# Tile 1's second halves: two pairs per copy, on ScalarE and GpSimd, and a reordered opening

## The chip, the cores and the metric

The kernel runs on one core of a Trainium2 chip. The metric is the device time of one execution in microseconds; lower is better. The engines are TensorE (PE, with its weight loads PEld), VectorE (DVE), ScalarE (ACT), GpSimd (POOL) and SyncE (SP). DMAs of this kernel that cast from float32 to bfloat16 are issued by POOL.

## The reference

Sliding-window causal attention feeds a SwiGLU block:

```
q, k, v: [8 batches, 8 heads, 576, 64]
scores = q k^T / 8, kept where 0 <= i - j < 64
x = softmax(scores) v, heads side by side: [4608 tokens, 512]
out = (silu(x @ w_gate) * (x @ w_val)) @ w_out     # d_ff = 1536
```

## The kernel before, in words

The 4608 tokens are worked in nine tiles of 512. Tiles 0 to 6 and 8 are the first 512 positions of a batch, tile 7 holds the last 64 positions of all eight batches. A tile goes through scores (`scores`, line 283), exp and masks (lines 296 to 304), sums (`totals`, 316), the mix with v (`mix`, 395), scaling by the inverse sums into `xT` (`scale`, 411), twelve gate and value steps m (`gate_value`, 455), each closed by a Silu on ScalarE and a product on VectorE into `hT` (`gate_end`, 448 and 449), and the projection (464). The projection of a tile is woven between the attention steps of the next. The order on each engine is written out by hand: the schedule is manual, and each engine runs its instructions in the order of the program text.

Heads are worked in four pairs u. Scores need queries and keys with the head dimension on the partitions. `turn_q` (221) and `turn_k` (231) make them by 32x32 block transposes on VectorE. For that, the second half (32 of 64 dimensions) of every row must lie on the next 32 partitions. For tile 2 and on, the loads themselves put it there by reading everything twice (`load_q`, `load_k`). For tile 1, `load_plain` (112, 118) reads once into partitions 0 to 31 and 64 to 95 (a = 0 and 1), and `second_halves` (132) copies the other half over, one pair and one a per copy: four pairs of k on ScalarE at m = 7 to 10, then q of pairs 0 and 1 on ScalarE and VectorE after the last m, and q of pairs 2 and 3 on VectorE after four projection columns.

Tile 0, the opening, is special: its q and k come through PE transposes, and its pairs are mixed by `mix_first` (361). That helper writes small marker matmuls (374), the first of them followed by a VectorE copy `seen` (378), between the parts of its accumulation. The order there is: mix pairs 0 to 2, scale pairs 0 and 1, first parts of pair 3, gate columns 0 and 1 for m = 0 and 1, the rest of pair 3, scale pairs 2 and 3, columns 2 and 3.

POOL's queue through the opening holds two casts and then only DMA issues: the gate and value weights (`weights_gv`, 195), tile 1's k and q between them, the output weights (`weights_o`, 201), tile 1's v (`load_halves`, 166), and then tile 2's loads. Around the change the program reads, after the last m of tile 0:

```
    scores(1, 0)
    columns(0, 4)
    for u in (2, 3):
        second_halves(1, "q", u, (on_v, on_v))
        turn_q(1, u)
    scores(1, 1)
    columns(4, 7)
```

`columns(c0, c1)` projects tile 0's rows of hT chunks c0 to c1 into four PSUM banks, the same banks that gate and value steps use.

Of the kernel before, what the change touches and what calls it, by code (L numbers as in the profile page):

```python
# [17 lines left out]
def kernel(  # L18
# [11 lines left out]
    S, D, H = 576, 64, 8  # L30
# [15 lines left out]
    bank = [two[i][:, j] for i in range(2) for j in range(2)]  # L46
# [58 lines left out]
    def load_plain(t, which, us):  # L105

        q_s, k_s = staged[t]
        for a in range(2):
            hs = slice(a + 2 * us.start, a + 2 * us.stop - 1, 2)
            r = slice(64 * a, 64 * a + 32)  # L110
            if which == "q":
                nc.gpsimd.dma_start(
                    q_s[r, us],
                    q[batch(t), hs, 0:512].rearrange("u (r e) d -> r u (e d)", e=16),
                )
            else:
                for u in range(us.start, us.stop):
                    nc.gpsimd.dma_start(
                        k_s[r, :, u],
                        k[batch(t), 2 * u + a, 0:512].rearrange("(g r e) d -> r g (e d)", g=4, e=4),  # L120
                    )

    def second_halves(t, which, u, copies):

        for a in range(2):
            src, dst = slice(64 * a, 64 * a + 32), slice(64 * a + 32, 64 * a + 64)
            if which == "q":
                ap = staged[t][0][:, u].rearrange("r (e d) -> r e d", d=D)
            else:
                ap = staged[t][1][:, :, u].rearrange("r g (e d) -> r g e d", d=D)  # L130
            half_d = (Ellipsis, slice(0, 32)), (Ellipsis, slice(32, 64))
            copies[a](ap[dst][half_d[0]], ap[src][half_d[1]])  # L132

    def load_k(k_s, groups):

# [64 lines left out]
    def weights_o(c0, c1):  # L200
        nc.gpsimd.dma_start(
            wo[:, c0:c1, :],
            moe_w_out[P * c0:P * c1].rearrange("(c r) f -> r c f", r=P),
        )
# [12 lines left out]
    def turn_q(t, u):  # L217

        if u == 0:
            queries[t] = att.tile([P, 4, 512], BF16, name="qT", tag="qT")  # L220
        nc.vector.transpose(  # L221
            queries[t][:, u, :].rearrange("r (e x) -> r e x", e=16),
            staged[t][0][:, u].rearrange("r (e d) -> r e d", d=D)[:, :, 0:32],
        )
# [5 lines left out]
    def turn_k(dst, k_s, u):  # L230
        nc.vector.transpose(  # L231
            dst[:, u, :].rearrange("r (g x e) -> r g e x", g=4, e=4),
            k_s[:, :, u].rearrange("r g (e d) -> r g e d", d=D)[:, :, :, 0:32],
        )
# [31 lines left out]
    def scores(t, w):  # L266

        qT = queries[t]
        s_ps = wide(), wide()
        for j in range(8):  # L270
            if t == LAST:
                k_j = kT[t % 2 if j < 4 else 2]
                pieces = [(j, j + 1, 0, k_j, P * (j % 4) + 64),
                          (j, j + 1, 1, k_j, P * (j % 4))]
            else:
                pieces = [(j, min(8, j + 2), 0, kT[t % 2], 64 * j)]
            for lo, hi, c, src, k0 in pieces:
                for h in range(2):
                    for x in range(2):
                        slot = s_ps[h][half(x)].rearrange("r a b -> r (a b)")  # L280
                        n = hi - lo
                        o = P * j + 64 * c
                        nc.tensor.matmul(  # L283
                            slot[:, o:o + 64 * n].rearrange(
                                "r (n e y) -> r e n y", n=n, e=16
                            ),
                            src[half(h), 2 * w + x, k0:k0 + 64],
                            blocks(qT[half(h), 2 * w + x], t, lo, hi).rearrange(
                                "r e (n y) -> r e n y", n=n
                            ),  # L290
                        )
        n = 1024 if t == LAST else 960
        for h in range(2):
            E = eb[2 * w + h]
            flat = E[:].rearrange("r s z -> r (s z)")[:, 64:64 + n]
            nc.scalar.activation(  # L296
                flat, s_ps[h][:].rearrange("r a b -> r (a b)")[:, 0:n], AF.Exp, scale=0.125
            )
            nc.vector.tensor_mul(  # L299
                flat, flat, mask[:].rearrange("r j c e y -> r (j c e y)")[:, 0:n]  # L300
            )
            both = epool.tile([P, 8, 64], BF16, name="both", tag="both")
            lo = 2 if t == LAST else 0
            nc.vector.tensor_add(both[:], E[:, 1:17:2], E[:, lo:lo + 15:2])  # L304
            weights[t, w, h] = E, both
# [49 lines left out]
    def mix_first(us, banks, mark):  # L355

        def part(u, o_ps, x, m):
            r = slice(0, P) if m % 2 else half(x)
            E = weights[0, u]
            for h in range(2):  # L360
                nc.tensor.matmul(
                    blocks(o_ps[half(h)], 0, m, m + 1),
                    v1[r, m // 2 if m % 2 or not x else m // 2 - 1, 2 * u + h, :],
                    blocks(E[r, h, :], 0, m, m + 1),
                    start=m + x == 0, stop=(m, x) == (6, 1),
                )

        def parts(x, ms):
            for u, b in zip(us, banks):
                for m in ms:  # L370
                    part(u, bank[b], x, m)

        def marker():
            nc.tensor.matmul(bank[mark][0:D, 0:16], ones[:, 0:D], ones[:, 0:16])

        parts(0, (0, 2, 4, 6))
        marker()
        nc.vector.tensor_copy(seen[:], bank[mark][0:D, 0:1])
        parts(0, (1, 3, 5, 7))
        yield  # L380
        marker()
        parts(1, (2, 4, 6))
# [21 lines left out]
    def scale(t, u, o_ps):  # L404
        if u == 0:
            xT[t] = att.tile([P, 4, 512], BF16, name="xT", tag="xT")
        x, r = xT[t][:, u, :], inverse.pop((t, u))
        if t == NT - 1:
            x, o_ps = x.rearrange("r (x e) -> r x e", e=16), turned(o_ps)
            r = r.rearrange("r (x e) -> r x e", e=16)  # L410
        nc.vector.tensor_mul(x, o_ps, r)  # L411
# [20 lines left out]
    def gate_part(t, ms, tiles, c):  # L432
        for m, pair in zip(ms, tiles):
            for ps, w in zip(pair, (wg, wv)):
                nc.tensor.matmul(
                    ps[:], w[:, c, P * m:P * m + P], xT[t][:, c, :],
                    start=(c == 0), stop=(c == 3),
                )
# [171 lines left out]
    q_s = stage.tile([P, 4, 16 * D], BF16, name="q_s", tag="q")  # L610
    k_s = stage.tile([P, 4, 4, 4 * D], BF16, name="k_s", tag="k")
    staged[1] = q_s, k_s
    load_plain(1, "k", slice(0, 2))
    weights_gv(1024, 1280)
    load_plain(1, "k", slice(2, 4))
    weights_gv(1280, 1536)
    load_plain(1, "q", slice(0, 2))
    weights_o(0, 4)
    load_plain(1, "q", slice(2, 4))
    weights_o(4, 8)  # L620
    weights_o(8, 12)
    load_halves(nc.gpsimd, vb[1], 1)
# [23 lines left out]
    scores_first(3)  # L646
    weigh_first(3)
    log2, inv2 = sums_first(2, 6)
    for _ in mix_first(range(3), (0, 1, 4), 7):
        pass  # L650
    log2()
    inv2()
# [1 line left out]
    log3()  # L654
    inv3()
    pairs = [(bank[2], bank[3]), (bank[0], bank[1])]
    for u in range(2):
        scale(0, u, bank[u])
    late = mix_first((3,), (5,), 6)
    next(late)  # L660
    for c in range(2):
        gate_part(0, (0, 1), pairs, c)
    for _ in late:
        pass
    for u in (2, 3):
        scale(0, u, bank[u + 2])
    for c in range(2, 4):
# [2 lines left out]
    for m in range(12):  # L670
        if m < 2:
            gate_end(0, m, pairs[m])
        else:
            gate_value(0, m)
        if m == 2:
            for x in range(2):
                for c in range(2):
                    nc.vector.tensor_copy(
                        mask[half(x), 0, c],
                        tri[half(x), x ^ c].rearrange("r (y e) -> r e y", e=16),  # L680
                    )
            for i in (1, 2, 4):
                nc.vector.tensor_copy(mask[:, i:2 * i], mask[:, 0:i])
            for E in eb:
                nc.vector.memset(E[:, 0], 0.0)
        if 7 <= m < 11:
            second_halves(1, "k", m - 7, (on_a, on_a))
            turn_k(kT[1], staged[1][1], m - 7)
    for u in range(2):
        second_halves(1, "q", u, (on_a, on_v))  # L690
        turn_q(1, u)

    set_exp()
    tiles = [out_tile(), d_tile(), out_tile(), d_tile()]
# [1 line left out]
    def columns(c0, c1):  # L696
        project_part(0, range(4), tiles, range(c0, c1))

    scores(1, 0)
    columns(0, 4)  # L700
    for u in (2, 3):
        second_halves(1, "q", u, (on_v, on_v))
        turn_q(1, u)
    scores(1, 1)
    columns(4, 7)
    for w in range(2):
# [79 lines left out]
```

## Time and profile before

| | |
|---|---|
| median of 3 runs | 331.77 us (331.74 to 332.35) |
| the profiled execution | 331.83 us, of which the trace spans 330.1 us |
| PE busy | 316.4 us (96%) |
| VectorE, ScalarE, GpSimd busy | 223.5, 170.5, 147.8 us |
| granted PE clock, whole span | 0.995 of full speed |

Engines run beside each other, so busy times do not add up. A line L of the profile is a line of the kernel; the helpers' lines gather all calls. In views by time, the first numbers are the start, in us from the start of the span, and the duration. "[1.07 <-DVE qT L221]" behind an instruction means that its engine had idled 1.07 us before it and that VectorE's instruction at line 221, which writes qT, ended that. Transfers issued by an engine are listed with the time from issue to landing.

### The profile page before, as it was taken

The numbers are of one execution on the slowest core, as the hardware profiler recorded it, in microseconds if no ns is written. First come the engines' busy times: TensorE is split into PE (matmuls) and PEld (weight loads), VectorE is DVE, ScalarE is ACT, GpSimd is POOL, SyncE is SP. The second block draws the span as 40 slices with busy tenths as digits, with TensorE's granted clock in tenths as the row PEclk, the third lists the DMA queues.
The fourth block names the chain that finished last, engine by engine and source line by source line (L and its number), as shares of the span: only waits on it lengthen the run. The fifth ranks groups of instructions, "written<-read, shape, count | busy, mean of one in ns | idle before, by whom it ended". The sixth has DMA issues, their size and how long they took to land.

```text
span 330.1 us, 6973 instructions
## 1 busy us (share of the span) xinstructions
PE 316.4 (96%) x2709; PEld 150.7 (46%) x2751; DVE 223.5 (68%) x353; ACT 170.5 (52%) x245; POOL 147.8 (45%) x264
## 2 busy tenths in 40 slices
PE   7999499999999999999999999999999999999995
PEld 3544244444544454444444454444444544444443
DVE  4765955588766776688669667875877666774332
ACT  5945836535743565356534663476337733683310
POOL 4959558955056579547603999375020000000000
PEclk9999979999999999999999999999999999999999
DMA  7999999997569998988990999799600300021013
GB/s 248 202 195 179 191 151 163 192 182 81 119 137 191 166 151 156 202 106 133 218 142 1 142 197 104 50 154 212 128 2 20 94 17 2 2 88 41 2 24 105
DMA packets 83602, 40.36 MB, mean 122 GB/s; under 512 B 64240, under 2 KB 78832, under 8 KB 83568
## 3 DMA queue, kind: packets, MB, share of 16 engines
q0 software_dynamic: 51568, 22.59, 57.6%
q1 hardware_dynamic: 31456, 16.79, 21.2%
q10 hardware_dynamic: 544, 0.52, 0.5%
q8 instruction: 21, 0.34, 0.4%
q14 instruction: 13, 0.11, 0.1%
HBM read 53.02 MB, written 9.44 MB: 189 GB/s over the span
## 4 chain that ended last, share of the span: by engine, by line
PE 84%; DMA 10%; POOL 3%; issue 1%; DVE 1%; SPq 0%; POOLq 0%
PE one L455 50%; PE one L464 27%; DMA wv<-in_moe_w_val_dram 4%; PE two L283 3%; DMA wo<-in_moe_w_out_dram 2%; PE two L395 2%; DMA vb<-in_v_dram 2%; DMA q_f<-in_q_dram 1%; PE one L316 1%; POOL wg L195 1%; PE one L506 1%; POOL wv L195 1%; POOL v L158 1%; DVE qT L221 0%; POOL qk_b L570 0%
## 5 line engine op out<-in xcount | busy, mean ns | idle before, releaser
L448 ACT ACTIVATE sg<-one 128x512 f32<-128x512 f32 x106 | 63.3, 597 | 109.5 <-PE one L455 82.2
L449 DVE TENSOR_TENSOR hT<-sg,one 128x512 bf16<-128x512 f32 x106 | 73.7, 695 | 57.1 <-PE one L455 56.2
L455 PE MATMUL one<-xT,wg 128*128 128x512 bf16 x416 | 108.4, 379 | 0.8
L455 PE MATMUL one<-xT,wv 128*128 128x512 bf16 x414 | 107.0, 379 | 0.1
L464 PE MATMUL one<-wo,hT 128*128 128x512 bf16 x397 | 95.1, 384 | 1.4 <-issue 0.3
L140 POOL DMA_DIRECT2D k_s<-in_k_dram x112 | 60.6, 554 | 25.7 <-DMA q_s<-in_q_dram 16.2
L455 PEld LDWEIGHTS <-wg 128*128 128x128 bf16 x424 | 41.5, 98 | 50.2 <-issue 0.3
L455 PEld LDWEIGHTS <-wv 128*128 128x128 bf16 x424 | 41.5, 98 | 50.0
L464 PEld LDWEIGHTS <-hT 128*128 128x128 bf16 x420 | 39.3, 98 | 47.8 <-issue 3.8
L231 DVE STREAM_TRANSPOSE kT<-k_s 128x512 bf16<-128x512 bf16 x32 | 41.3, 1292 | 0.5 <-ACT k_s L132 0.3
L296 ACT ACTIVATE eb<-two 128x960 bf16<-128x960 f32 (+1 forms) x32 | 29.5, 974 | 20.9 <-PE two L283 20.8
L299 DVE TENSOR_TENSOR eb<-eb,mask 128x960 bf16<-128x960 bf16 (+1 forms) x32 | 21.5, 672 | 15.5 <-ACT eb L296 15.5
L191 POOL CAST vb<-v_f 128x512 bf16<-128x512 f32 x20 | 11.5, 621 | 38.4 <-PE one L455 23.5
L411 DVE TENSOR_TENSOR xT<-two,r 128x512 bf16<-128x512 f32 x34 | 21.7, 686 | 6.4 <-PE two L395 4.8
L333 ACT ACTIVATE r<-r 128x512 f32<-128x512 f32 (+1 forms) x34 | 22.3, 655 | 1.0
L221 DVE STREAM_TRANSPOSE qT<-q_s 128x512 bf16<-128x512 bf16 x32 | 22.6, 705 | 0.3
L330 ACT ACTIVATE r<-one 128x512 f32<-128x512 f32 x32 | 18.9, 591 | 5.3 <-PE one L316 4.7
L91 POOL DMA_DIRECT2D q_s<-in_q_dram x24 | 13.2, 560 | 6.1 <-DVE qT L221 5.1
L283 PE MATMUL two<-qT,kT 64*64 64x128 bf16 (+1 forms) x576 | 10.7, 212 | 4.9 <-DVE qT L221 4.9
L304 DVE TENSOR_TENSOR both<-eb 128x512 bf16<-128x512 bf16 x32 | 13.6, 425 | 1.1
L166 POOL DMA_DIRECT2D vb<-in_v_dram x16 | 11.0, 716 | 6.5 <-DMA wo<-in_moe_w_out_dram 6.4
L283 PEld LDWEIGHTS <-kT 64*64 64x64 bf16 x576 | 8.4, 106 | 11.7 <-issue 11.3
(114 smaller groups left out, 198.1 us busy)
## 6 DMA issues: line engine op xcount, KB each, us to landing
k_s<-in_k_dram POOLq DMA_DIRECT2D x112, 56.0 KB, 4.5
q_s<-in_q_dram POOLq DMA_DIRECT2D x24, 248.0 KB, 5.8
v_f<-in_v_dram SPq DMA_DIRECT2D x40, 128.0 KB
wo<-in_moe_w_out_dram POOLq DMA_DIRECT2D x3, 512.0 KB, 10.0
wg<-in_moe_w_gate_dram POOLq DMA_DIRECT2D x5, 256.0 KB, 6.5
wv<-in_moe_w_val_dram POOLq DMA_DIRECT2D x5, 256.0 KB, 6.6
q_f<-in_q_dram SPq DMA_DIRECT2D x4, 256.0 KB
vb<-in_v_dram POOLq DMA_DIRECT2D x16, 64.0 KB, 6.0
```

Source lines behind the costliest of these rows:

```text
L140: nc.gpsimd.dma_start(k_s[p0:p0 + 32, g, :, 0:w], k[b, a:H:2, s:s + P].rearrange("u (r e) d -> r u (e d)", e=4) [:, :, 32 * c:32 * c + w],)
L221: nc.vector.transpose(queries[t][:, u, :].rearrange("r (e x) -> r e x", e=16), staged[t][0][:, u].rearrange("r (e d) -> r e d", d=D)[:, :, ...
L231: nc.vector.transpose(dst[:, u, :].rearrange("r (g x e) -> r g e x", g=4, e=4), k_s[:, :, u].rearrange("r g (e d) -> r g e d", d=D)[:, :, ...
L283: nc.tensor.matmul(slot[:, o:o + 64 * n].rearrange("r (n e y) -> r e n y", n=n, e=16), src[half(h), 2 * w + x, k0:k0 + 64], blocks(qT[half ...
L296: nc.scalar.activation(flat, s_ps[h][:].rearrange("r a b -> r (a b)")[:, 0:n], AF.Exp, scale=0.125)
L299: nc.vector.tensor_mul(flat, flat, mask[:].rearrange("r j c e y -> r (j c e y)")[:, 0:n])
L333: nc.scalar.activation(r, r, AF.Exp, scale=-1.0)
L411: nc.vector.tensor_mul(x, o_ps, r)
L448: nc.scalar.activation(sg[:], g_ps[:], AF.Silu)
L449: nc.vector.tensor_mul(hT[t][:, m, :], sg[:], v_ps[:])
L455: nc.tensor.matmul(ps[:], w[:, c, P * m:P * m + P], xT[t][:, c, :], start=(c == 0), stop=(c == 3),)
L464: nc.tensor.matmul(o_ps[:], hT[t][:, c, P * s:P * s + P], wo[:, c, :], start=(c == 0), stop=(c == 11),)
```

## The change

- `second_halves` copies two pairs at once, for one a per call: 32 partitions x 1024 elements. For k and for q of pairs 0 and 1, a = 1 is done by GpSimd, in its queue among the DMA issues, and a = 0 by ScalarE after the Silu of m = 5 (k of pairs 0, 1), 7 (q of pairs 0, 1) and 9 (k of pairs 2, 3). The last, q of pairs 2, 3, is done by VectorE.
- The loads come in the order k of pairs 0, 1; q of 0, 1; k of 2, 3; q of 2, 3, woven otherwise with the weights. The first output weights come in two DMAs.
- Turns: k at m = 6, 8, 11 and after; q of pairs 0, 1 at m = 9, 10. After the last m, VectorE turns k of pair 3, copies q of pairs 2, 3 and turns them. One projection column then precedes the first scores, three follow.
- In the opening, only pairs 0 and 1 are mixed first, pair 2 goes with pair 3, and the second scale and the gate columns move.

```diff
-    def second_halves(t, which, u, copies):
...
+    def second_halves(t, which, us, a, copy):
+
+        src, dst = slice(64 * a, 64 * a + 32), slice(64 * a + 32, 64 * a + 64)
+        if which == "q":
+            ap = staged[t][0][:, us].rearrange("r u (e d) -> r (u e) d", d=D)
+        else:
+            ap = staged[t][1][:, :, us].rearrange("r g u (e d) -> r g (u e) d", d=D)
+        copy(ap[dst][..., 0:32], ap[src][..., 32:64])
...
-    load_plain(1, "k", slice(0, 2))
+    lo, hi = slice(0, 2), slice(2, 4)
+    load_plain(1, "k", lo)
     weights_gv(1024, 1280)
-    load_plain(1, "k", slice(2, 4))
+    load_plain(1, "q", lo)
+    second_halves(1, "k", lo, 1, on_p)
     weights_gv(1280, 1536)
-    load_plain(1, "q", slice(0, 2))
-    weights_o(0, 4)
-    load_plain(1, "q", slice(2, 4))
+    load_plain(1, "k", hi)
+    second_halves(1, "q", lo, 1, on_p)
+    weights_o(0, 2)
+    weights_o(2, 4)
+    load_plain(1, "q", hi)
+    second_halves(1, "k", hi, 1, on_p)
     weights_o(4, 8)
     weights_o(8, 12)
     load_halves(nc.gpsimd, vb[1], 1)
...
-    for _ in mix_first(range(3), (0, 1, 4), 7):
+    for _ in mix_first(range(2), (0, 1), 7):
...
-    for u in range(2):
-        scale(0, u, bank[u])
-    late = mix_first((3,), (5,), 6)
+    scale(0, 0, bank[0])
+    late = mix_first((2, 3), (4, 5), 6)
     next(late)
-    for c in range(2):
-        gate_part(0, (0, 1), pairs, c)
+    scale(0, 1, bank[1])
+    gate_part(0, (0, 1), pairs, 0)
     for _ in late:
         pass
+    gate_part(0, (0, 1), pairs, 1)
...
-        if 7 <= m < 11:
-            second_halves(1, "k", m - 7, (on_a, on_a))
-            turn_k(kT[1], staged[1][1], m - 7)
-    for u in range(2):
-        second_halves(1, "q", u, (on_a, on_v))
-        turn_q(1, u)
+        if m in (5, 7, 9):
+            which, us = {5: ("k", lo), 7: ("q", lo), 9: ("k", hi)}[m]
+            second_halves(1, which, us, 0, on_a)
+        if m in (6, 8, 11):
+            turn_k(kT[1], staged[1][1], {6: 0, 8: 1, 11: 2}[m])
+        if m in (9, 10):
+            turn_q(1, m - 9)
...
+    turn_k(kT[1], staged[1][1], 3)
+    for a in range(2):
+        second_halves(1, "q", hi, a, on_v)
+    for u in (2, 3):
+        turn_q(1, u)
+    columns(0, 1)
     scores(1, 0)
-    columns(0, 4)
-    for u in (2, 3):
-        second_halves(1, "q", u, (on_v, on_v))
-        turn_q(1, u)
+    columns(1, 4)
     scores(1, 1)
     columns(4, 7)
```

More of the change, by code (lines that the diff above doesn't have):

```diff
@@ L121, in load_plain @@
                     )
-    def second_halves(t, which, u, copies):
[L125 to L132, printed above, removed]
+    def second_halves(t, which, us, a, copy):
[5 more added lines that the diff above has]
+        copy(ap[dst][..., 0:32], ap[src][..., 32:64])
     def load_k(k_s, groups):
```

## The prediction

> **What bounds the kernel now.** The page first: PE is busy for 316.4 of 330.1 us, and from 57.7 us on the chain that ended last is PE work almost without a break, some 34 us for each tile. What can be won lies where PE is not busy, so the table of windows came next. Its columns are the window and its length, busy us (and instructions) of PE, PEld, DVE, ACT and POOL, PE's granted clock, DMA share, GB/s:
>
> ```profile
> 37.10:39.90 2.80, 0.00 (x0) 0.00 (x1) 2.68 (x4) 2.76 (x4) 1.70 (x3) 1.00 1.20 204
> 39.90:41.20 1.30, 0.21 (x1) 0.10 (x1) 1.15 (x3) 0.10 (x1) 0.35 (x1) 1.00 1.24 200
> 41.50:44.90 3.40, 3.40 (x34) 1.36 (x23) 1.80 (x4) 1.83 (x2) 1.13 (x2) 0.50 1.90 172
> 46.90:48.60 1.70, 0.94 (x34) 0.66 (x34) 0.98 (x2) 0.00 (x0) 0.65 (x2) 1.00 0.89 100
> 48.60:57.70 9.10, 8.89 (x102) 4.05 (x105) 4.19 (x8) 6.48 (x8) 7.81 (x15) 1.00 1.17 168
> ```
>
> PE does nothing from 37.1 to 39.9 and almost nothing until 41.2, then runs 3.4 us at half clock, and idles once more before 48.6. The timeline of PE and then of ACT and DVE there (start, us, instruction, idle before it) says for what:
>
> ```profile
> 36.04 0.81 PE L455 MATMUL one<-xT,wv 128*128 128x512 bf16 x3
> 41.24 0.79 PE L283 MATMUL two<-qT,kT 64*64 64x128 bf16 x31 [1.07 <-DVE qT L221]
> 41.96 5.08 PE L464 MATMUL one<-wo,hT 128*128 128x512 bf16 x16
> 47.97 0.62 PE L283 MATMUL two<-qT,kT 64*64 64x128 bf16 x31 [0.76 <-DVE qT L221]
> ```
> ```profile
> 37.57 1.14 ACT L132 COPY q_s<-q_s 32x512 bf16<-32x512 bf16 x2
> ```
> ```profile
> 38.08 0.71 DVE L449 TENSOR_TENSOR hT<-sg,one 128x512 bf16<-128x512 f32 x1
> 38.82 0.28 DVE L132 COPY q_s<-q_s 32x512 bf16<-32x512 bf16 x1
> 39.20 0.71 DVE L221 STREAM_TRANSPOSE qT<-q_s 128x512 bf16<-128x512 bf16 x1
> 39.94 0.43 DVE L132 COPY q_s<-q_s 32x512 bf16<-32x512 bf16 x1
> 40.48 0.71 DVE L221 STREAM_TRANSPOSE qT<-q_s 128x512 bf16<-128x512 bf16 x1
> ```
>
> Gate work of tile 0 ends at about 37.07 (a fourth matmul of the x3 row is not recorded). The first scores of tile 1 need the turned queries of pairs 0 and 1. These come from ACT copies at 37.57 and DVE copies and turns that end at 41.2. Pairs 2 and 3 come last at 47.92. So from 37.07 to the end of both scores at 48.59, 11.5 us, PE does 0.55 + 16 x 0.216 + 0.55 = 4.6 us of work. The other 7 us: 2.9 + 1.07 idle, half of 3.41 at half clock (1.7), 1.0 before the second scores, gaps.
>
> **The opening.** Finishing the mix of pairs 0, 1 first takes pair 2's 22 matmuls (some 0.02 each) out of the way of DVE's first scale, which starts about 0.4 earlier (14.79 now). But the second scale stands behind a marker copy that waits for the first parts of pairs 2 and 3: scale to 15.1, marker copy to 15.4, scale to 16.07, as now. Gate column 0 of m = 1 waits for it in both. Behind it PE does column 0 to 16.55, the late parts to 16.85, column 1 to 17.7 (the scales of 2 and 3 end at 18.35 beside it), columns 2 and 3 to 19.47: m = 2 starts there for 19.64 now, 0.17 earlier. Bounds: 0.4 gained (the whole lead kept) to 0.3 lost (the 0.34 PE idles before that scale).
>
> **Loads and POOL's copies.** The view of a tile, cut down to one issue, gives the landing; for the last k load:
>
> ```profile
> L118 POOL DMA_DIRECT2D k_s<-in_k_dram x1: 545/545/545, 26.3 to 26.3; - x1
> DMA to landing us min/median/max: 3.8/3.8/3.8
> ```
>
> So it lands at 30.1. Read so for all, POOL issues a load when the eighth before it has landed, and loads land one after the other, at these spacings: 0.30 us for a k load, 0.64 q, 1.28 and 1.55 for wg and wv, 2.57 for a 512 KB wo, 0.42 vb. Bytes are the same, wo(0, 4) is split in two (one issue more, 0.8 us of POOL). The cost is that three copies now sit in the queue that issues the loads, each waiting for its own load, with everything behind it waiting too: copy k of pairs 0, 1 holds wg/wv of 1280; copy q holds wo(0, 2); copy k of 2, 3 holds wo(4, 8), the rest of wo and vb. No row shows a GpSimd copy to other partitions, and none could make it a gain, since it is added. The nearest is its cast of 128x512, 618 ns; twice the elements make 1.24, and I take 1.2. Ends: 0.62 (half-size elements at no cost) to 2.5 (twice over for short runs and the partition shift); ACT's 615 ns for a shifted 32x512 against 587 for a plain 128x512 copy says that a shift need not cost much. Walking the queue with these: k of 0, 1 lands at 26.05 as now (19.50 + 6.55), copy 26.4 to 27.6; q of 0, 1 lands at 30.3; wg and wv of 1280 at 31.6 and 33.1 (now 31.4, 32.9; needed at 33.3 and 34.1); copy q 31.3 to 32.5; k of 2, 3 at 34.3; copy 35.2 to 36.4; wo(0, 2) at 35.9, wo(2, 4) at 37.2, q of 2, 3 at 38.5. Three or four loads stay outstanding during each wait, and that hides the waits. Without that cover each copy costs the queue its whole length.
>
> **ACT.** Ten copies of 0.615 go, three of 32x1024 come; the 128x1024 rows on ACT (1.02 to 1.06) price them at 1.04. Each follows a Silu with 1.13 idle behind it, so the next Silu is hardly late. Only the third waits (for k at 33.4 to 33.7) and makes the Silu of m = 10 0.4 late, with a double buffer behind it.
>
> **DVE from m = 6.** k and q turns (1.33 and 0.71) of pairs 0, 1 move between the products hT, where the trace has about 1.04 idle each; products run up to 0.4 late and the PSUM pairs absorb it. After the last product (37.0 to 37.7, no longer kept by a turn and a late Silu): two k turns 2.66, two copies 32x1024, two q turns 1.42. A 32x512 copy took 283 ns; doubled 0.57, two 1.14; ends 0.83 (fixed part once) and 1.9, as the copy at 39.94 took 0.43 beside POOL's issues and the q cast at 8.58 took 0.79 for 0.42. With 0.2 of gaps the last turn ends at 43.1.
>
> The Trainium skill (SBUF — State Buffer, "Who interferes with whom") has VectorE's two-port copies and GpSimd exclude each other for a whole instruction. The 0.43 and 0.79 us rows agree in direction but are far short of a full block. By that rule two copies behind vb issues of 0.68 would end 0.8 later, and the total would be 328.3.
>
> **PE.** Gate work ends at 36.9. `columns(0, 1)` now stands ahead of the scores and its fourth matmul waits for the last product: to 37.97. Scores to 38.5, `columns(1, 4)` 12 x 0.216 to 41.1. Then PE waits for the q turns until 43.1: 2.0 idle, where it now idles 2.9 + 1.07 and loses 1.7 to the clock. The trace shows full clock through the 2.8 us window and half clock only behind it, so I charge nothing here. Second scores end at 43.65, 4.94 earlier than 48.59.
> The Trainium skill (TensorE: Matmul & The Clock Gate, "The HAM clock gate") gives a free-running window of about 3.4 us; 2.0 idle is inside it, and were the clock lost all the same, 1.7 would come back.
>
> What is late next: DVE's masks of both pairs, 2.14 each (49.62 to 51.76 now). Those of the first scores now stand behind the q turns, 43.1 to 45.25, the second set ends at 47.4. `columns(4, 7)` and the first totals end at 46.7, so PE waits 0.7 for what cost 0.1 to 0.2 before: 0.6 given back. From there the order is as now.
>
> **Sum.** 4.94 (opening's 0.17 in it) - 0.6 = 4.3. The profiled execution took 331.83 us (span 330.1 and 1.7 around it), 0.06 above the median of the runs, 331.77. Forecast 331.8 - 4.3 = 327.5. Each tile after it is paced by PE, so the shift lasts.
>
> **Rivals.**
> *Slower: GpSimd's copies are long.* Up to 1.65 us each they are hidden; beyond, three excesses less 1.3 of slack delay the k turns of pairs 2, 3 and all behind. At 2.0 each: 3 x 0.8 - 1.3 = 1.1, 328.6. At about 2.5 the wait reaches 2.0 + 2.6 = 4.6 us, as long as now's idle, the half clock (1.7) returns and the gain is gone. At 3.0: 3 x 1.8 - 1.3 + 1.7 = 5.8, 333.3. For it: no row of such a copy. Against: 618 ns for 512 elements.
> *Given back at tile 2.* Its k loads landed up to 61.74 and DVE turned them at 67.88; that turn moves to about 63.6, and the output writes of tile 0 (57.7 to 63) move into these loads. If they slip 2 to 3 us, DVE's turn holds the products behind it: 0.5 to 2 back, 328 to 329.5.
> *It only moves the wait* (q of 2, 3 late or blocked copies): PE idles over 3 us and pays the clock, 329.5 to 330.5.
>
> **Chances.** Forecast, 326.6 to 328.4: 0.63. Copies of 1.65 to 2.5 us: 0.12. Given back at tile 2: 0.10. Wait moved: 0.06. Slower: 0.06. No change: 0.03. The range runs from 326.5 (gain 5.3: opening 0.4, copies 0.83, no wait at the totals) to 329.7 (into the second and third cases). A measurement of this kernel tells 0.2%, 0.66 us, from no change: faster 0.91, same 0.03, slower 0.06.
>
> **What would show it.** Right: no half clock after 5 us, ACT copies near 1.04, POOL copies near 1.2, first scores near 38, last q turn near 43, second scores then, gate work of tile 1 near 53.4 (57.74 now), and turns of tile 2 that wait for no load. Wrong: a POOL copy over 1.65, a k turn at line 229 that waits for POOL, half clock near 43, or products of tile 1 held by a turn.

## The result and the profile after

The changed kernel took 327.67 us, median of four runs (327.35 to 328.41), beside 332.00 (331.74 to 332.35) for the kernel before on the same chip: ratio 0.9872, interval 0.9851 to 0.9893. The profiled execution took 327.35 us, its span 325.6; before it was 331.83 and 330.1, so 4.48 less. The forecast was 327.5.

The table of windows over the four stretches where PE stood before (columns as in the prediction):

```profile
37.10:39.90 2.80, 2.66 (x42) 1.10 (x40) 2.38 (x4) 2.04 (x3) 2.57 (x5) 1.00 1.07 160
39.90:41.20 1.30, 1.30 (x7) 0.59 (x6) 1.27 (x2) 1.30 (x2) 1.15 (x2) 1.00 1.17 181
41.50:44.90 3.40, 2.56 (x41) 1.24 (x40) 3.30 (x7) 1.12 (x2) 0.68 (x1) 1.00 1.53 189
46.90:48.60 1.70, 1.48 (x9) 0.61 (x7) 0.27 (x1) 1.67 (x2) 1.56 (x3) 1.00 1.08 74
```

PE works 7.99 of these 9.2 us, for 4.55 before, and its clock column holds no 0.50. In exchange VectorE now works almost without a gap from 37.7 until its masks end at 47.2. The timeline of PE from the last gate work of tile 0 (start, us, instruction, idle before it and what ended it), then that of VectorE:

```profile
37.73 1.08 PE L462 MATMUL one<-wo,hT 128*128 128x512 bf16 x4
38.74 0.62 PE L281 MATMUL two<-qT,kT 64*64 64x128 bf16 x32
39.29 2.76 PE L462 MATMUL one<-wo,hT 128*128 128x512 bf16 x12
42.55 0.24 PE L281 MATMUL two<-qT,kT 64*64 64x128 bf16 x1 [0.49 <-DVE qT L219]
43.14 0.61 PE L281 MATMUL two<-qT,kT 64*64 64x128 bf16 x31 [0.35 <-DVE qT L219]
47.22 0.40 PE L314 MATMUL two<-both,ones 64*64 64x512 bf16 x2 [0.22 <-DVE both L302]
```
```profile
37.69 0.69 DVE L447 TENSOR_TENSOR hT<-sg,one 128x512 bf16<-128x512 f32 x1 [0.42 <-PE one L453]
38.30 2.47 DVE L229 STREAM_TRANSPOSE kT<-k_s 128x512 bf16<-128x512 bf16 x2
40.80 0.95 DVE L130 COPY q_s<-q_s 32x1024 bf16<-32x1024 bf16 x2
41.78 1.30 DVE L219 STREAM_TRANSPOSE qT<-q_s 128x512 bf16<-128x512 bf16 x2
```

Both scores of tile 1 are now kept only by what VectorE has left after the last product: the first by the product itself (the fourth matmul of `columns(0, 1)`, ahead of them, writes the PSUM bank that this product reads; it starts at 38.43, behind the product's end at 38.38), the second by two k turns, two copies and two q turns in a row. The second scores end at 43.75 (48.59 before).

The unknown price of the prediction was the GpSimd copy. Its rows, with one of ScalarE's (timeline of each):

```profile
26.02 1.03 POOL L130 COPY k_s<-k_s 32x1024 bf16<-32x1024 bf16 x1 [0.53 <-DMA k_s<-in_k_dram]
30.67 1.09 POOL L130 COPY q_s<-q_s 32x1024 bf16<-32x1024 bf16 x1
34.13 1.11 POOL L130 COPY k_s<-k_s 32x1024 bf16<-32x1024 bf16 x1
27.02 1.04 ACT L130 COPY k_s<-k_s 32x1024 bf16<-32x1024 bf16 x1
```

Executions differ in when the opening gets going: its last scores (pair 3) start between 12.19 and 12.90 in the profiles of this study, 12.52 before and 12.90 after. These instructions lie ahead of everything the change touches. Below, stretches are therefore counted from that start, called the mark. The timeline of PE there, before and after:

```profile
12.52 0.41 PE L254 MATMUL two<-qT,kT 64*64 64x128 bf16 x16 [0.55 <-DVE kT L212]
```
```profile
12.90 0.41 PE L252 MATMUL two<-qT,kT 64*64 64x128 bf16 x16 [0.55 <-DVE kT L210]
```

| stretch | before | after | difference |
|---|---|---|---|
| mark to the end of tile 1's second scores | 12.52 to 48.59, 36.07 | 12.90 to 43.75, 30.85 | -5.22 |
| from there to gate work of tile 1 | to 57.74, 9.15 | to 53.15, 9.40 | +0.25 |
| from there to the first scores of tile 2 | to 78.55, 20.81 | to 74.45, 21.30 | +0.49 |
| mark to the last projection (324.03, 319.92) | 311.51 | 307.02 | -4.49 |

What was won at one place, 5.2, was partly given back at two others; the rest of the kernel passes on -4.5. Of the 5.22, 0.79 are won ahead of the end of tile 0's last product (26.27 after the mark before, 25.48 now) and 4.43 behind it. The later start of the opening (+0.38) and a shorter tail behind the last projection (5.68 for 6.07) cancel in this execution.

### The profile page after: what moved, and what is told of

It reads as the page before. It is cut to its first block, busy times and chain, and to the rows that moved or that the text cites. A ratio compares the mean times of both kernels' runs of the same rounds, so it can differ in the third digit from the quotient of the medians.

```text
span 325.6 us, 7013 instructions
## 1 busy us (share of the span) xinstructions
PE 318.7 (98%) x2751; PEld 150.6 (46%) x2751; DVE 221.4 (68%) x349; ACT 167.5 (51%) x238; POOL 151.3 (46%) x268
## 4 chain that ended last, share of the span: by engine, by line
PE 92%; DVE 4%; DMA 2%; ACT 1%; issue 0%; ACTq 0%; DVEq 0%
PE one L453 56%; PE one L462 27%; PE two L281 2%; PE two L393 2%; DMA k_f<-in_k_dram 2%; PE one L314 1%; PE two L433 1%; PE one L504 1%; DVE kT L229 1%; DVE eb L297 1%; DVE both L302 1%; DVE qT L219 0%; DVE kT L210 0%; PE one L307 0%; ACT eb L582 0%
## 5 line engine op out<-in xcount | busy, mean ns | idle before, releaser
L453 PE MATMUL one<-xT,wv 128*128 128x512 bf16 x424 | 108.8, 379 | 0.3 <-DVE hT L447 0.3
L91 POOL DMA_DIRECT2D q_s<-in_q_dram x24 | 13.1, 564 | 4.3 <-DVE qT L219 4.0
L98 POOL DMA_DIRECT2D q_s<-in_q_dram x16 | 8.6, 597 | 7.0 <-DVE qT L219 6.4
```

The lines of the kernel that those rows point to most:

```text
L453: nc.tensor.matmul(ps[:], w[:, c, P * m:P * m + P], xT[t][:, c, :], start=(c == 0), stop=(c == 3),)
```

## Experiments

**The theories.** Mine: the time is set by VectorE's chain behind the last product of tile 0. The change turns q of pairs 0 and 1 ahead of that product, and q of pairs 2 and 3 ahead of the masks of the first scores; two k turns move behind the product in exchange, and PE has columns to do meanwhile. Rivals: the opening's reorder brings it; the full clock brings it (a separate 1.7 us of the prediction's seven); GpSimd's share of the copies, or the new order of the loads, brings it.

### The opening's reorder, alone and taken out

The first kernel is the one before with only the opening of the changed one; the second is the changed kernel with the opening of before:

```diff
-    for _ in mix_first(range(3), (0, 1, 4), 7):
+    for _ in mix_first(range(2), (0, 1), 7):
...
-    for u in range(2):
-        scale(0, u, bank[u])
-    late = mix_first((3,), (5,), 6)
+    scale(0, 0, bank[0])
+    late = mix_first((2, 3), (4, 5), 6)
...
```

> The kernel before with the opening's reorder alone (mix of pairs 0, 1 first, pair 2 with pair 3, the second scale and the gate columns moved). Forecast's step: m = 2 starts 0.17 us earlier, -0.2 us in all. What the changed kernel's trace suggests: its first scores of pair 3 were 0.38 late against before for a reason ahead of the reorder (12.90 against 12.52), and m = 2 was 0.52 late (20.16 against 19.64), so the reorder itself costs 0.14: time of before +0.1. Rival: the whole 0.5 belongs to the reorder: +0.5.

> The changed kernel with the old opening. If the second halves, loads and turns carry the gain, it stays within 0.4 us of the changed kernel (327.3 to 327.8). If the opening mattered by more than its bounds (0.4 gained, 0.3 lost), it falls outside 327.0 to 328.1.

Alone it gave 332.35 us beside 332.16, ratio 1.0011 (0.9999 to 1.0023). Taken out it left 327.56, ratio 0.9870 (0.9853 to 0.9887), as good as the whole change. PE's timeline of the kernel with the reorder alone, from the mark to m = 2:

```profile
12.30 0.41 PE L254 MATMUL two<-qT,kT 64*64 64x128 bf16 x16 [0.55 <-DVE kT L212]
19.55 1.03 PE L455 MATMUL one<-xT,wg 128*128 128x512 bf16 x4
```

From mark to m = 2 it is 7.25 here and 7.26 in the changed kernel (12.90 to 20.16), but 7.12 in the kernel before (12.52 to 19.64) and 7.12 with the old opening (12.55 to 19.67). The reorder costs 0.13 to 0.14. It is no part of the gain.

### The half clock

Ten matmuls on constants are put into the idle stretch of the kernel before, ahead of tile 1's first scores; nobody reads their result:

```diff
+    for _ in range(10):
+        nc.tensor.matmul(bank[0][0:D], ones[:, 0:D], ones[:])
     scores(1, 0)
     columns(0, 4)
```

> The kernel before with ten matmuls of 0.216 us into an unused bank between tile 0's last gate step and the first scores, so PE's idle is 2 us for 4 and the clock should stay full from 41.5 to 44.9. If the half clock was a term of the loss, as the forecast's list has it: -1.7 us, 330.2. If VectorE's chain (first scores, exp, masks, q copies and turns up to 47.92) sets the second scores whatever the projection columns take, the half clock was hidden: within 0.3 us of before, 331.7 to 332.0.

It took 331.98 us, ratio 0.9990 (0.9973 to 1.0008). The window that had shown 0.50, and PE's second scores:

```profile
41.50:44.90 3.40, 3.28 (x43) 1.76 (x44) 1.67 (x4) 1.83 (x2) 1.11 (x2) 1.00 1.87 173
```
```profile
46.80 0.24 PE L283 MATMUL two<-qT,kT 64*64 64x128 bf16 x1 [1.06 <-DVE qT L221]
48.19 0.61 PE L283 MATMUL two<-qT,kT 64*64 64x128 bf16 x31 [1.16 <-DVE qT L221]
```

The clock stayed full, the columns were done earlier, and PE waited longer for the same query turn: the second scores begin at 48.19, for 47.97 before; counted from the marks (12.72 and 12.52) that is 35.47 and 35.45. This half clock was a symptom that lay beside VectorE's chain. As the cause of the gain, the rival falls.

The runs of the kernel before leave a smaller question open. Of the 29 beside these experiments, 15 had a mean granted clock of 0.993 to 0.995, as in the trace, with a median of 331.57; 14 had 0.988 to 0.990, with a median of 332.36. No trace shows where the second group lost more clock. The ten runs with the extra matmuls that kept 0.999 or 1.000 have a median of 331.70, so removing the stretch of the trace won nothing, but some tenths of the changed kernel's median gain may go with the other loss; the two traced executions, 4.48 apart, are both without it.

### GpSimd's share: three times, and none

First each of the three GpSimd copies is done three times over (the edit of one):

```diff
-    second_halves(1, "k", lo, 1, on_p)
+    for _ in range(3):
+        second_halves(1, "k", lo, 1, on_p)
...
```

> The changed kernel with each of GpSimd's three copies done three times over, so some 3.2 us for 1.08. Theory (GpSimd's copies hold the loads behind them and the turns that wait for them, hidden only up to about 1.65 us each): k of pairs 2, 3 is copied at about 42 for 35.2, the k turns wait for it some 4 us, the clock drops again: 331.5 to 333.5. Rival (three or four loads outstanding hide the copies at any such length): 327.5 to 328.5.

It took 331.97 us, ratio 1.0012 (0.9990 to 1.0034): the whole gain is gone, at 3.23 to 3.29 us per set (the profiled execution 333.32). The timeline of POOL, VectorE and PE there:

```profile
38.62 3.28 POOL L130 COPY k_s<-k_s 32x1024 bf16<-32x1024 bf16 x3
41.93 2.48 DVE L229 STREAM_TRANSPOSE kT<-k_s 128x512 bf16<-128x512 bf16 x2 [2.00 <-POOL k_s L130]
35.83 1.04 PE L453 MATMUL one<-xT,wv 128*128 128x512 bf16 x4 [1.24 <-DMA wv<-in_moe_w_val_dram]
39.84 1.04 PE L462 MATMUL one<-wo,hT 128*128 128x512 bf16 x4 [1.25 <-DMA wo<-in_moe_w_out_dram]
46.49 0.24 PE L281 MATMUL two<-qT,kT 64*64 64x128 bf16 x1 [2.36 <-DVE qT L219]
```

So the slower rival was a real one with about the right place: the turns wait for POOL at line 229, and the weights behind the copies in the queue come late as well (wv, wo). It did not decide because a copy takes 1.1 us and not 2.5.

Then GpSimd has none (the three calls go; one is shown), and ScalarE does both a, one behind the other, after the same Silus:

```diff
-    second_halves(1, "k", lo, 1, on_p)
...
-            second_halves(1, which, us, 0, on_a)
+            for a in range(2):
+                second_halves(1, which, us, a, on_a)
```

> The changed kernel without GpSimd's copies: ScalarE does both a, so two copies of 1.04 us each time. ScalarE's Silu of m = 6, 8, 10 come some 1 us late, the last product about 0.4, and with it the turns: 327.8 to 328.3. If GpSimd's part is what carries the gain: above 329. If three copies in the queue of the loads cost something: below 327.2.

Measured 327.20 us, ratio 0.9859 (0.9845 to 0.9874). I had expected 327.8 to 328.3 from late Silus; that missed. ScalarE's rows and PE's:

```profile
26.99 2.11 ACT L130 COPY k_s<-k_s 32x1024 bf16<-32x1024 bf16 x2
36.03 1.29 ACT L446 ACTIVATE sg<-one 128x512 f32<-128x512 f32 x2
```
```profile
38.59 0.38 PE L462 MATMUL one<-wo,hT 128*128 128x512 bf16 x1 [0.39 <-DVE hT L447]
```

Silus run back to back at 36.03 and the last product is late by 0.39 for PE, but the second scores start 30.39 after the mark, for 30.24 in the changed kernel: 0.15. On the other side POOL's queue runs freer. The timeline of POOL at the first output weights, in the changed kernel and in this one, then the windows of both, 33 to 35 us:

```profile
31.65 1.46 POOL L199 DMA_DIRECT2D wo<-in_moe_w_out_dram  x2
```
```profile
29.80 1.42 POOL L199 DMA_DIRECT2D wo<-in_moe_w_out_dram  x2
```

```profile
33.00:35.00 2.00, 2.00 (x11) 0.88 (x9) 2.00 (x4) 1.64 (x2) 2.00 (x4) 1.00 1.12 130
```
```profile
33.00:35.00 2.00, 2.00 (x11) 0.87 (x9) 1.79 (x3) 1.85 (x4) 1.71 (x3) 1.00 1.24 198
```

With GpSimd's copies 130 GB/s move, without them 198, and the first output weights, issued 1.85 later, land at 37.68 and 35.49. GpSimd's share is not needed. The two intervals overlap, so the times do not say that it harms; a delay of tile 2's loads that goes with it is shown below.

### Where the 0.7 went that was given back

*Turns of tile 2 one to two steps later* (of the changed kernel, nothing else):

```diff
-        turns = (4, 6, 8, 10) if t == 1 else (1, 4, 7, 10)
+        turns = (5, 7, 9, 11) if t == 1 else (1, 4, 7, 10)
```

> The changed kernel with tile 2's turns one step later (m = 5, 7, 9, 11 of tile 1 for 4, 6, 8, 10). In the changed kernel's trace the first k turn of tile 2 waited 1.32 us for loads that landed at 64.4, and PE lost some 0.7 behind it. If that is 0.7 us given back at tile 2: 327.0, and no k turn waits for a load. Rival (the loss is hidden elsewhere, or a turn at m = 11 holds tile 2's scores): 327.6 or more.

It took 327.09 us, ratio 0.9847 (0.9834 to 0.9860), an interval that still overlaps that of the changed kernel. The timeline of VectorE and PE in the changed kernel and in the one with the old opening, and of VectorE in this one:

```profile
64.68 1.34 DVE L229 STREAM_TRANSPOSE kT<-k_s 128x512 bf16<-128x512 bf16 x1 [1.32 <-DMA k_s<-in_k_dram]
66.59 1.02 PE L453 MATMUL one<-xT,wv 128*128 128x512 bf16 x4 [0.33 <-DVE hT L447]
```
```profile
65.35 1.33 DVE L229 STREAM_TRANSPOSE kT<-k_s 128x512 bf16<-128x512 bf16 x1 [2.17 <-DMA k_s<-in_k_dram]
67.25 1.02 PE L453 MATMUL one<-xT,wv 128*128 128x512 bf16 x4 [1.17 <-DVE hT L447]
```
```profile
64.39 1.33 DVE L229 STREAM_TRANSPOSE kT<-k_s 128x512 bf16<-128x512 bf16 x1
```

VectorE's turn waits for tile 2's last k load, the product behind it is late, and PE waits for that product. In the later order the wait is gone, and gate work to tile 2's first scores takes 20.82 (52.48 to 73.30), as before the change. Five executions of kernels with the early turns show how one wait becomes the other:

| kernel | VectorE waits for k | PE waits for the product |
|---|---|---|
| ScalarE does all copies | 0.96 | 0 |
| columns 4 to 8 (below) | 1.18 | 0.18 |
| changed kernel | 1.32 | 0.33 |
| scores first (below) | 1.68 | 0.68 |
| changed, old opening | 2.17 | 1.17 |

PE loses, to 0.01, what is over 1.0. The load itself landed at 64.40 in the changed kernel (61.74 before). Between 48 and 64 us the outputs of tile 0 now move 1.05 MB for 0.70 before: they are issued from 53.1 to 58.6, for 57.7 to 63.1. That these writes hold the loads up is what the prediction's second rival says. But about half of the delay is older than they are: tile 2's first q load lands at 51.06 for 49.71, 1.35 late, before the first write is issued. It was issued late, since POOL's queue ahead of it was late. The timeline of POOL before (a view that ends at 47) and after:

```profile
44.45 0.68 POOL L166 DMA_DIRECT2D vb<-in_v_dram  x1 [1.92 <-DMA wo<-in_moe_w_out_dram]
45.31 1.70 POOL L91 DMA_DIRECT2D q_s<-in_q_dram  x3 [0.18 <-DVE both L304]
```
```profile
46.02 0.68 POOL L164 DMA_DIRECT2D vb<-in_v_dram  x1 [2.10 <-DMA vb<-in_v_dram]
47.04 2.17 POOL L91 DMA_DIRECT2D q_s<-in_q_dram  x4 [0.34 <-DVE eb L297]
```

This late start goes with GpSimd's copies: in the five profiles with all three of them, each done once, that load is issued at 47.04 to 48.30; in the four descendants of the changed kernel with one or none (ScalarE does all copies, and the last three versions below) at 44.37 to 45.81. The other half fits the writes. From the landing of the first q load to that of the last k load it takes 12.03 before, and 10.96 and 11.72 in the two variants of the kernel before; in the changed kernel 13.35, and 12.39 to 14.00 in its eight variants without tripled copies. No run moved the writes alone.

*Columns 4 to 8 ahead of the sums*, one more than now:

```diff
-    columns(4, 7)
+    columns(4, 8)
...
-    columns(7, 10)
+    columns(8, 10)
```

> The changed kernel with projection columns 4 to 8 ahead of the sums and 8 to 10 behind them (4 to 7 and 7 to 10 before). The second totals waited for VectorE's masks at about 46.8 to 47.2; one column more covers that, and then ScalarE's logarithm holds the mix: 0.3 to 0.4 gained, 327.3. Rival (the wait at the totals costs nothing, the mix is set by ScalarE alone): within 0.15 of the changed kernel, 327.5 to 327.8.

It took 327.27 us, ratio 0.9858 (0.9843 to 0.9873). The totals wait no more, but the mix behind them does:

```profile
47.42 0.63 PE L314 MATMUL two<-both,ones 64*64 64x512 bf16 x8
50.96 0.61 PE L393 MATMUL two<-eb,vb 64*64 64x128 bf16 x32 [0.53 <-ACT r L328]
```

The column came from the place that covered the inverse sums. Its interval overlaps that of the changed kernel; no gain is shown.

*Scores ahead of all four columns*:

```diff
-    columns(0, 1)
     scores(1, 0)
-    columns(1, 4)
+    columns(0, 4)
```

> The changed kernel with the first scores of tile 1 ahead of all four projection columns, as before. First scores then start near 37.5 for 38.74. If VectorE's chain of turns up to 43 alone sets the second scores: no change, 327.4 to 327.9. If the order of columns and scores carries part of the gain: 328.2 or more; if the column in front was a cost, 327.0 or less.

It took 327.90 us, ratio 0.9883 (0.9859 to 0.9907): no difference. The timeline of PE:

```profile
37.30 0.97 PE L281 MATMUL two<-qT,kT 64*64 64x128 bf16 x32
42.96 0.61 PE L281 MATMUL two<-qT,kT 64*64 64x128 bf16 x31 [0.35 <-DVE qT L219]
```

The first scores start at once, at 37.30, and the second ones 30.27 after the mark, for 30.24: they wait for VectorE as before.

### Shorter chains: a version that beats both

*Joined*: the changed kernel with the old opening (as above), ScalarE in GpSimd's place, the later turns of tile 2, and columns in other pieces:

```diff
-            second_halves(1, which, us, 0, on_a)
+            for a in range(2):
+                second_halves(1, which, us, a, on_a)
...
-    columns(4, 7)
+    columns(4, 8)
...
-    columns(7, 10)
+    columns(8, 11)
...
-    columns(10, 12)
+    columns(11, 12)
...
-        turns = (4, 6, 8, 10) if t == 1 else (1, 4, 7, 10)
+        turns = (5, 7, 9, 11) if t == 1 else (1, 4, 7, 10)
```

> The changed kernel without GpSimd's copies (ScalarE does both a), with the old opening, tile 2's turns at m = 5, 7, 9, 11, projection columns 4 to 8 ahead of the sums, 8 to 11 ahead of the mix and 11 to 12 behind it. If the single gains add (0.5, 0.1, 0.6, 0.4): 326.1. If tile 2's loads, free to land at 64.2 anyway, and VectorE's chain swallow part: 326.4 to 327.0.

It took 326.60 us beside 331.71, ratio 0.9853 (0.9834 to 0.9873), a smaller gain than the sum of the parts (326.1). VectorE's chain is the same, so the second scores come 30.22 after the mark, as in the changed kernel; and one column is too little to hide the scaling of tile 1:

```profile
53.52 0.38 PE L453 MATMUL one<-xT,wg 128*128 128x512 bf16 x1 [0.22 <-DVE xT L409]
```

The next two go for VectorE's chain itself, by two ways with nothing else in common. *q early*: joined, with q of pairs 2, 3 loaded ahead of the output weights and its copies off VectorE, so that only the four turns are left (and the first scores ahead of all four columns):

```diff
     load_plain(1, "k", hi)
+    load_plain(1, "q", hi)
     weights_o(0, 2)
     weights_o(2, 4)
-    load_plain(1, "q", hi)
     weights_o(4, 8)
+    second_halves(1, "q", hi, 1, on_p)
     weights_o(8, 12)
...
+        if m == 11:
+            second_halves(1, "q", hi, 0, on_a)
...
-    for a in range(2):
-        second_halves(1, "q", hi, a, on_v)
...
```

> The joined kernel with q of pairs 2, 3 loaded ahead of the output weights, copied by GpSimd (a = 1, in its queue ahead of the last output weights) and ScalarE (a = 0, after the Silu of m = 11), and scores ahead of the projection columns. VectorE's chain after the last product loses its two copies (0.95): second scores near 42.2, 0.5 to 0.9 below the joined kernel. Rival: the output weights land 1.3 us later and PE waits for them ahead of the columns: no gain or 0.5 above it.

*k, then q*: joined with the loads in the order of before (all of k, then q), k turned at m = 6 to 9 and q of pairs 0, 1 at m = 10, 11, so that two copies and the turns of q are left but no turn of k (the loads are not shown):

```diff
...
-            which, us = {5: ("k", lo), 7: ("q", lo), 9: ("k", hi)}[m]
+            which, us = {5: ("k", lo), 7: ("k", hi), 9: ("q", lo)}[m]
...
-        if m in (6, 8, 11):
-            turn_k(kT[1], staged[1][1], {6: 0, 8: 1, 11: 2}[m])
-        if m in (9, 10):
-            turn_q(1, m - 9)
+        if 6 <= m < 10:
+            turn_k(kT[1], staged[1][1], m - 6)
+        if m in (10, 11):
+            turn_q(1, m - 10)
...
-    turn_k(kT[1], staged[1][1], 3)
```

> The joined kernel with the loads' old order (all k, then q of 0, 1, then q of 2, 3), k of pairs 2, 3 copied at m = 7 and q of 0, 1 at m = 9, k turns at m = 6 to 9, q turns of 0, 1 at m = 10, 11. If what matters is how much VectorE has left after the last product (here one q turn, two copies, two q turns: 3 us for the joined kernel's 5), the second scores come near 41.9, 1.0 to 1.3 below the joined kernel. If q's earlier load is what the gain needs, the q turns wait for loads at 34.2 and it is no faster than the joined kernel.

They took 325.66 us (ratio 0.9817, 0.9803 to 0.9831) and 325.92 (0.9828, 0.9813 to 0.9843). The timeline of VectorE and PE, first of *q early*, then of *k, then q*:

```profile
40.62 1.29 DVE L219 STREAM_TRANSPOSE qT<-q_s 128x512 bf16<-128x512 bf16 x2
42.01 0.62 PE L281 MATMUL two<-qT,kT 64*64 64x128 bf16 x32
```
```profile
38.72 1.07 DVE L130 COPY q_s<-q_s 32x1024 bf16<-32x1024 bf16 x2
39.83 1.30 DVE L219 STREAM_TRANSPOSE qT<-q_s 128x512 bf16<-128x512 bf16 x2
41.98 0.62 PE L281 MATMUL two<-qT,kT 64*64 64x128 bf16 x32
```

In both the last turn is done ahead of the second scores, to which PE comes straight from its columns: 29.11 and 29.47 after the mark, for 30.22 joined. Both are faster than the joined kernel by about what its PE had waited there (0.42 + 0.35, and gaps), 0.94 and 0.68. The interval of *k, then q* still touches that of joined (up to 0.9843, from 0.9834), but in the traces the last projection starts 306.48 after the mark joined, 305.39 in *q early* and 305.75 in *k, then q*. One of them takes k and q of pairs 0, 1 first and uses GpSimd, the other takes all of k first and uses no GpSimd. So neither order nor engine is what counts, but the work left to VectorE behind the last product: 2.47 + 0.95 + 1.30 in the changed kernel, down to 2.45 + 1.29 or 0.68 + 1.07 + 1.30. This is what my theory says, and the rivals do not. It holds only as far as PE waits: in *k, then q* VectorE is done at 41.13, 0.85 ahead of the scores, and nothing more is won by that. Not taken apart by any run is what, within the changed kernel, turning q of pairs 0 and 1 ahead of the product brings, what turning q of pairs 2 and 3 ahead of the masks, and what the fewer, longer copies. *q early* is the best version found, 6.05 us below the kernel before on its chip.

## Why the prediction was right, point by point

**The opening** was wrong in sign: 0.17 earlier by the sum, 0.13 to 0.14 later by the runs, inside the bounds. Counted from the mark, the first scale starts 0.13 earlier (2.14 for 2.27), where "about 0.4 earlier" was said; the first column of m = 1 starts at 3.70, for 3.55 forecast (16.07) and 3.61 before; and from there to m = 2 it is 3.56 for 3.40, mostly because the late parts, with pair 2 in them now, take 0.43 (17.12 to 17.55) for 0.30. The 0.15 and 0.16 are the whole miss.

**POOL's copies**: 1.03 to 1.11 us for 1.2, well inside 0.62 to 2.5. The landings up to k of pairs 2, 3 were as forecast or up to half a microsecond earlier (25.85, 29.80, 31.1, 32.7, 33.94). The step of the prediction that failed here is "three or four loads stay outstanding during each wait, and that hides the waits": wo(0, 2) landed at 37.68 for 35.9, wo(2, 4) at 38.72 for 37.2, q of pairs 2, 3 at up to 40.03 for 38.5, and without the copies wo(0, 2) came at 35.49. It was issued at 31.65 and took 6.0 us to land, while the loads then outstanding were through at 33.94. It cost next to nothing here only because VectorE needs that q at 40.80, and because the fourth matmul of the first column waits for the last product (38.38) anyway. What it did cost came later: it was part of the delay of tile 2's loads, which the prediction put down to the output writes alone.

**VectorE's chain**, the term that carries the forecast, ended at 43.08 for 43.1. It started 0.7 late (last product 37.69 for 37.0, from the opening and its mark) and was shorter by as much: k turns 2.47 for 2.66, copies 0.95 for 1.14, q turns 1.30 for 1.42, 0.5 together, and the rest in its gaps. The chain was the right one, but that its end was hit to 0.02 is luck, as the two misses cancelled. Pairs of equal turns cost 0.1 to 0.2 less than two single ones.
For the two copies the Trainium skill's exclusion (SBUF — State Buffer, "Who interferes with whom") would have added 0.8 by the prediction's estimate, to about 1.9. The runs show no such full block: the two copies took 0.87 where POOL issued nothing beside them (joined), 0.95 where it issued loads up to 41.05 (the changed kernel), and 0.92 to 1.32 in all profiles with issues beside them.

**PE**: the first scores ended at 39.36 for 38.5, the columns behind them at 42.05 for 41.1, so the wait for the q turns was 0.84 for 2.0. The end is the same (43.75 for 43.65), since VectorE sets it.

**The clock**: "the other 7 us" counted 1.7 for the half clock as lost time. The gain did not need it: the run with the clock held full brought nothing. The sum did not rest on that term, as it was made from the end of the chain, and so came out right.
The rule of the Trainium skill (TensorE: Matmul & The Clock Gate, "The HAM clock gate") that the clock falls after idling agrees in direction: no half clock where PE idles 0.84, and 3.4 us of it behind the long idle before (PE busy 0.27 of 38.1 to 41.3). With the tripled copies half clock came although PE had been busy 0.85 of 45.1 to 48.3, so the idle stretch need not be empty.

**Given back at the totals**: 0.25 for 0.6. VectorE was done with the masks at 47.2 for 47.4, and PE came to wait for them only at 47.0 for 46.7, as its columns ended later: 0.22 and not 0.7.

**Gate work of tile 1** thus starts 4.59 earlier, for 4.3. **Tile 2** then gave back 0.49, which the forecast put into a rival at 0.10: it happened in part, with loads 2.7 us later and a PE wait of 0.33 here, up to 1.17 in another kernel (old opening). The two misses, +0.35 at the totals and -0.49 at tile 2, nearly cancel: the mechanism of the gain was right, and that the total came within 0.2 us is in part luck. "Each tile after it is paced by PE, so the shift lasts" held from tile 2 on: 4.1 at its first scores and 4.1 at the last projection.

**The slower rival** was priced too high: at 3.0 us each 333.3 was forecast; at 3.25 the median is 331.97. Its formula at 3.25, 3 x 2.05 - 1.3 + 1.7 above 327.5, gives 334.05, and without the 1.7 for the half clock 332.35. The ten runs speak for such a term: the four with a mean clock of 0.999 or 1.000 took 330.69 to 332.06, the four with 0.994 or 0.995 (one of them profiled, with half clock from 48.6 to 51.9) 331.87 to 333.32, the two with 0.990 333.96 and 334.37. So even at full clock the formula is about 1 us too high, and why is open.

## What to carry to other kernels

Where a second engine prepares the operands of the next stage, find the last result of the present stage on that engine and add up what it still has to do behind it: shortening this sum is what a change can win here, down to where the waiting engine's own work sets the pace; its clock alone won nothing. Work that can be moved ahead of that result is worth moving by any engine and in any order of loads that brings it there. A shift of several microseconds also moves output writes into loads that had slack before, and compute work in the queue that issues loads makes even later loads start late, so look for the first wait that this creates and move that instruction too.

## What the runs showed of the hardware

- A GpSimd copy of 32x1024 bfloat16 to other partitions takes 1.03 to 1.11 us, ScalarE's 1.04, VectorE's 0.44 to 0.66 (two took 0.87 to 1.32).
- GpSimd copies in the queue that issues the loads thin out the transfers behind them: 130 GB/s with, 198 without, and output weights issued 1.85 and landed 2.2 us later. The next tile's first load was issued at 47.04 to 48.30 with three such copies, at 44.37 to 45.81 with one or none.
- A stretch at half clock can cost nothing: ten extra matmuls removed it, ratio 0.9990 (0.9973 to 1.0008). In another kernel (tripled copies) runs with less clock were longer, 331.87 to 334.37 for 330.69 to 332.06.
